# Chunk 0's denominators from one matmul, chunk 3's second score products halved on VectorE, a last column piece of 128, and a new order of the steps

## The chip, the cores and the metric

The kernel runs on one core of one Trainium2 chip. A core has five engines with queues of their own: TensorE (PE, matmuls, and PEld for its weight loads), VectorE (DVE), ScalarE (ACT), GpSimd (POOL) and SyncE (SP). The last two mainly issue transfers here; ACT issues one as well. The metric is device time in microseconds of one launch. Before the change it is 195.9 us, the median of three runs (195.79 to 197.63).

## The reference

One transformer layer over 2048 positions of width 512, all in bfloat16:

```
h  = x + Attn(layernorm(x))            # 32 heads of 16
h2 = h + MLP(layernorm(h))             # 512 -> 1376 -> 512
Attn: q,k,v = x @ wqkv;  each position sees 8 positions: itself and 2, 4, .. 14 back
      logits = q*k summed over a head's 16 numbers, times 1/4; softmax over the 8; sum of p*v; @ wo
MLP:  relu(x @ W_gate) * (x @ W_up) @ W_down
```

A position before the first one is masked out. The output is h2.

## The kernel before

The 2048 positions are cut into four chunks (0 to 3) of 512. Within a chunk a step has a name, which the plan's code gives it (the first argument of `add`); here it is written name/chunk, for instance pr1/3.

- **Norm and projections.** xst, xag, xxn and their like make the first layer norm, xtp transposes on PE (xtd by a transfer). qkv0 to qkv11 are the projections, four matmuls of 512 columns each (line 572), and qe0 to qe11 (line 580) copy the banks out on ACT. Chunk 0's first six are cut into qka, qkb, qkc.
- **Scores.** pr0 and pr1 (line 620; the digit is the half hf: the near four or the far four of the eight positions) multiply q by the shifted k on DVE, 128x4096 at a time: one such tile holds two of the four t (a head's 16 numbers lie as 4 partitions by 4 tiles t), four shifts each. There are two of them for each half. sc0 and sc1 (line 628) sum over a head's numbers with the 128x32 matrix `sel`, sixteen matmuls per half: four column groups of the array times four t. ex0 and ex1 (line 696) take exp on ACT, mk masks in chunk 0.
- **Denominators.** In chunks 1 to 3 (`DEN1`) es (line 728) adds the two halves' exponentials on DVE and den is one matmul with `same` (line 713); in chunk 0 den is two matmuls with `spread`, one for each half, that add up in the bank (line 716). dl and dr (lines 719, 722) are ln and exp(-x) on ACT, which make the reciprocal. In chunks 1 to 3 am0 and am1 (line 740) multiply the exponentials by it; in chunk 0 the division comes later (om, line 795).
- **Weighted sums.** bd0 and bd1 (line 756) spread the weights over the partitions, four transfers each, in SP's queue. mu0 to mu3 (line 788, in chunk 0 line 803) multiply by v on DVE, ta (line 831) adds the upper half to the lower by a transfer that POOL issues, in chunks 0 to 2; tree (lines 791, 825) adds the rest on DVE, in chunk 3 all of it.
- **Output projection and second norm.** wo0 to wo3 (line 867) are four matmuls for 128 positions each, rs (line 878; in chunk 0 line 876 on ACT) adds the residual, hsq, hrl, hre and hxn make the second layer norm, htp transposes on PE, htd by transfers in SP's queue.
- **MLP.** mm0 to mm4 (line 940) are the gate and up projections, four groups of four matmuls in each, mm5 (line 907) the last 96 columns. ue and ge (lines 944, 947) copy out on ACT, gu (line 968) multiplies on DVE, gtd transposes the last piece. dn0 to dn3 (line 990) are the down projections of 128 positions each, in two parts: hidden tiles 0 to 7, then 8 to 10. o (line 1003, on ACT for chunks 0 and 1: line 999) evicts them, os (lines 1009, 1027) stores them from SP's queue; in chunks 0 and 1 oa (line 1024) adds to the residual by a transfer of POOL's first.
- **The last block.** In chunk 3 the last 128 positions are computed in column pieces (`LASTC`, lines 975 to 978): columns 0 to 255 (dn3) and 256 to 511 (dn4). Only the very last piece is stored from ACT's queue (lines 1006 to 1009).

All banks of PSUM are one pool of eight (line 294), the 4096-wide tiles one of five, the `gr` and `up_sb` tiles two each.

**What sets the order.** Each call of `add` numbers a step in the order of creation, and `RANK[number]` (lines 18 to 57) is its rank: each engine does its steps in the order of rank (lines 119 to 123). The planner (`Plan.order`) walks these queues with a duration for each step and chooses which buffer a step takes; the program is then written out in that order. So every engine works strictly down its list, and a step that waits holds back all that stand behind it on its engine.

Of the kernel before, what the change touches and what calls it, by code (L numbers as in the profile page):

```python
# [17 lines left out]
RANK = [  # L18
# [38 lines left out]
]  # L57


# [33 lines left out]
class Plan:  # L93
# [9 lines left out]
    def add(self, key, *a, **k):  # L103
        op = Op(*a, **k)
        op.key = key
        op.seq = len(self.ops)
        if RANK:
            op.prio = RANK[op.seq]
        self.ops.append(op)
        for b in set(op.take) | set(op.use):  # L110
            b.left += 1
        return op
# [90 lines left out]
def kernel(  # L203
# [12 lines left out]
    Bsz, S, D = A_x.shape  # L216
# [5 lines left out]
    W = 8  # L222
    DIL = 2
    PADL = 16
    DEN1 = (1, 2, 3)
    BCD = {(0,0):"SSSS",(0,1):"SSSS",(1,0):"SSSS",(1,1):"SSSS",(2,0):"SSSS",(2,1):"SSSS",(3,0):"SSSS",(3,1):"SSSS"}
    PRE = ()
    PRD = ()
    PRH = {}
    ODA = (0, 1)  # L230
    LATE = "ud"
    NAB = 0
# [64 lines left out]
    V = nc.vector  # L297
# [94 lines left out]
    HSP = ()  # L392
    TMT = (0, 1, 2, 3)
    TTM, DTG, ATE = 0.0845, 0.35, 0.3
    LASTC = (D // 2,)

    LNA = ((0, 1, 0, 1), (0, 0, 0, 0))

# [156 lines left out]
    for tk in range(NCK):  # L555
# [50 lines left out]
        for hf in range(2):  # L606
            sc, ex = Buf(at_s), Buf(ex_s)
            scd, prd = [], []
            for t in range(0, NT, 2):
# [12 lines left out]

                hs = PRH.get((tk, hf, t))

# [62 lines left out]
            elif tk in MERGE:  # L687
                scd = [add(("sc%d" % hf, tk), "PE", (4 - sum((tk, hf, t) in PRH for t in (0, 2))) * MM + SW, lambda p=prd: [f() for _, _, f in p],
                           [a for a, _, _ in prd], apr, take=[sc], use=[b for _, b, _ in prd], lat=PEL)]
# [21 lines left out]
        def f_dn(exs=exs, dn=dn, tk=tk, es=None):  # L711
            if tk in DEN1:
                nc.tensor.matmul(dn.t[:], lhsT=(same if tk in EARLY else spread)[:], rhs=es.t[:], start=True, stop=True)  # L713
                return
            for hf in range(2):
                nc.tensor.matmul(dn.t[:], lhsT=(same if tk in EARLY else spread)[:], rhs=exs[hf].t[:], start=(hf == 0), stop=(hf == 1))  # L716
# [6 lines left out]

        if tk in DEN1:
            es = Buf(es_s)
# [250 lines left out]
        if tk == NCK - 1:  # L976
            cs = (0,) + LASTC + (D,)
            parts[-1:] = [(BPC - 1, a, b) for a, b in zip(cs, cs[1:])]
# [98 lines left out]
```

## Time and profile before

| what | value |
|---|---|
| median of three runs | 195.9 us |
| the profiled execution's own time | 196.0 us |
| its span | 193.7 us, at the full clock throughout |
| PE busy | 188.5 us (97%) |
| DVE busy | 147.2 us (76%) |
| ACT busy | 115.2 us (59%) |
| POOL busy | 17.4 us (9%) |

The span is what the profiler recorded; 2.3 us of the execution lie around it. The page cuts the span into 40 slices of 4.84 us. Busy shares are means over stages: the chain of waits says which engine's work ended last in each. A matmul's listed duration (379 ns for 512 columns) overlaps its neighbours'; what a matmul takes is read from a run of them in the chain. A vector instruction too is listed some 0.08 us longer than the distance to its successor.

### The profile page before, as it was taken

How to read it: one execution, taken by the hardware profiler on the slowest of the kernel's cores; microseconds unless marked ns; L12 is line 12 of the kernel's file. 1: busy time of each engine (PE TensorE's matmuls, PEld its weight loads, DVE VectorE, ACT ScalarE, POOL GpSimd, SP SyncE). 2: the span in 40 equal slices, each digit the busy share in tenths (PEclk: the TensorE clock that was granted, in tenths of full speed). 3: DMA queues.
4: the chain of work that ended last, by engine and by line, in shares of the span. 5: the costliest groups of instructions: out<-in, count | busy, mean ns of one | idle time of the engine just before them, and what ended most of it. 6: DMA issues, size and time to landing. Idle time of an engine off the chain costs nothing.

```text
span 193.7 us, 3083 instructions
## 1 busy us (share of the span) xinstructions
PE 188.5 (97%) x1120; PEld 99.0 (51%) x1139; DVE 147.2 (76%) x239; ACT 115.2 (59%) x241; POOL 17.4 (9%) x35
## 2 busy tenths in 40 slices
PE   7999999999999999999999999999999999999993
PEld 7986455555436435454444554444445444545452
DVE  6889999999999999999997679999564401134331
ACT  3489898965999673965156649623478712435500
POOL 3000002330000013100044001003000000000000
PEclk9999999999999999999999999999999999999999
DMA  6799564999902609917579974135101624001102
GB/s 205 242 296 376 138 155 93 192 196 260 353 5 49 171 14 199 191 33 170 122 143 194 180 192 90 29 80 94 18 0 27 162 58 135 0 27 54 30 23 86
DMA packets 25070, 24.61 MB, mean 127 GB/s; under 512 B 11136, under 2 KB 21344, under 8 KB 25056
## 3 DMA queue, kind: packets, MB, share of 16 engines
q1 hardware_dynamic: 22032, 16.23, 30.1%
q0 software_dynamic: 2304, 7.34, 20.8%
q10 hardware_dynamic: 720, 0.85, 1.2%
q8 instruction: 9, 0.15, 0.3%
q14 instruction: 5, 0.04, 0.1%
HBM read 8.42 MB, written 2.10 MB: 54 GB/s over the span
## 4 chain that ended last, share of the span: by engine, by line
PE 97%; ACT 1%; issue 1%; DVE 0%; ACTq 0%
PE bank L940 35%; PE bank L572 21%; PE bank L990 20%; PE bank L867 7%; PE bank L628 4%; PE bank L421 3%; PE bank L907 3%; PE bank L531 2%; PE bank L429 1%; ACT up_sb L944 1%; PE bank L870 0%; PE bank L713 0%; PE bank L716 0%; DVE row L1003 0%; ACT vT L580 0%
## 5 line engine op out<-in xcount | busy, mean ns | idle before, releaser
L940 PE MATMUL bank<-quad,wgu_sb 128*128 128x512 bf16 x312 | 72.4, 379 | 0.4
L940 PEld LDWEIGHTS <-wgu_sb 128*128 128x128 bf16 x320 | 31.0, 98 | 36.4 <-issue 1.0
L990 PE MATMUL bank<-wd_sb,gT 128*128 128x512 bf16 (+2 forms) x185 | 39.6, 366 | 0.1
L944 ACT CAST up_sb<-bank 128x512 bf16<-128x512 f32 x40 | 22.3, 590 | 22.2 <-PE bank L940 20.5
L572 PE MATMUL bank<-quad,wqk_sb 128*128 128x512 bf16 (+1 forms) x148 | 29.4, 344 | 0.3
L947 ACT ACTIVATE gr<-bank 128x512 bf16<-128x512 f32 x40 | 23.5, 606 | 9.5 <-PE bank L940 5.2
L968 DVE TENSOR_TENSOR gT<-gr,up_sb 128x1024 bf16<-128x1024 bf16 x20 | 13.8, 688 | 19.4 <-ACT up_sb L944 10.5
L990 PEld LDWEIGHTS <-gT 128*128 128x128 bf16 (+1 forms) x187 | 18.2, 98 | 19.8 <-DVE gT L968 0.2
L620 DVE TENSOR_TENSOR big<-quad,kT 128x4096 bf16<-128x4096 bf16 x12 | 27.2, 2284 | 0.2 <-ACT kT L580 0.2
L788 DVE TENSOR_TENSOR big<-big,vT 128x4096 bf16<-128x4096 bf16 x12 | 27.1, 2285 | 0.2 <-PE bank L940 0.2
L572 PEld LDWEIGHTS <-wqk_sb 128*128 128x128 bf16 x152 | 16.7, 113 | 10.3 <-issue 0.2
L831 POOL DMA_DIRECT2D big<-big x12 | 10.5, 904 | 81.7 <-DVE big L788 54.2
L791 DVE TENSOR_TENSOR big<-big 128x1024 bf16<-128x1024 bf16 (+2 forms) x24 | 16.9, 728 | 0.0
L572 PE MATMUL bank<-quad,wv_sb 128*128 128x512 bf16 x61 | 15.3, 380 | 0.2
L867 PE MATMUL bank<-wo_sb,quad 128*128 128x512 bf16 x62 | 15.0, 379 | 0.1
L1003 DVE TENSOR_TENSOR row<-x_sm,bank 128x512 bf16<-128x512 bf16 (+1 forms) x9 | 5.5, 627 | 12.2 <-PE bank L990 12.2
L456 ACT ACTIVATE row<-x_sm,mv 128x512 bf16<-128x512 bf16 x12 | 8.6, 718 | 7.2 <-DVE mv L448 7.1
L547 ACT COPY quad<-bank 128x1024 bf16<-128x1024 bf16 (+1 forms) x10 | 8.6, 898 | 7.2 <-PE bank L531 7.2
L878 DVE SCALAR_TENSOR_TENSOR x_sm<-x_sm,bank 128x512 bf16<-128x512 bf16 x12 | 8.2, 687 | 4.9 <-PE bank L867 4.7
L580 ACT CAST kT<-bank 128x512 bf16<-128x512 f32 x16 | 9.1, 597 | 3.3 <-PE bank L572 1.8
L467 DVE BATCH_NORM_STATS2 st<-x_sm 128x6 f32<-128x512 bf16 x16 | 10.2, 675 | 0.4 <-DMA x_sm<-in_A_x_dram 0.4
L580 ACT CAST quad<-bank 128x512 bf16<-128x512 f32 x16 | 9.5, 602 | 1.6 <-PE bank L572 1.5
(77 smaller groups left out, 169.5 us busy)
## 6 DMA issues: line engine op xcount, KB each, us to landing
big<-big POOLq DMA_DIRECT2D x12, 512.0 KB, 5.3
big<-ex SPq DMA_DIRECT2D x32, 128.0 KB, 2.8
wgu_sb<-in_B_W_gate_dram SPq DMA_DIRECT2D x2, 688.0 KB, 7.7
wgu_sb<-in_B_W_up_dram SPq DMA_DIRECT2D x2, 688.0 KB, 7.5
wd_sb<-in_B_W_down_dram SPq DMA_DIRECT2D x2, 640.0 KB, 7.9
x_sm<-in_A_x_dram SPq DMA_DIRECT2D x2, 512.0 KB, 5.1
x_sm<-up_sb POOLq DMA_DIRECT2D x4, 256.0 KB, 3.8
out_dram<-x_sm SPq DMA_DIRECT2D x4, 256.0 KB, 2.3
```

Of the source, the lines that this page charges most:

```text
L572: nc.tensor.matmul(mm.t[:, lo:hi], lhsT=wv_sb[:, dt, t:D:NT] if c == 2 else wqk_sb[:, dt, c * D + t:(c + 1) * D:NT], rhs=xnT.t[:, dt, lo:h ...
L580: nc.scalar.copy(out=o, in_=mm.t[:])
L620: V.tensor_tensor(out=pb.t[:].rearrange("p (t w) s -> p t w s", t=2), in0=q4, in1=k4, op=ALU.mult)
L788: V.tensor_tensor(out=mt.t[:], in0=ab.t[:], in1=v8, op=ALU.mult)
L791: V.tensor_tensor(out=mt.t[:, 0:n, :], in0=mt.t[:, 0:n, :], in1=mt.t[:, n:2 * n, :], op=ALU.add)
L831: nc.gpsimd.dma_start(mt.t[:, 0:4, :], mt.t[:, 4:8, :], accum_op=ALU.add)
L867: nc.tensor.matmul(od.t[:], lhsT=OT.t[:, t, j * P:(j + 1) * P], rhs=wo_sb[:, t, :], start=(t == 0), stop=(t == NT - 1 and tk not in RPE))
L940: nc.tensor.matmul(mm.t[:fs, lo:hi], lhsT=wgu_sb[:, dt, g, ft * P: ft * P + fs], rhs=hnT.t[:, dt, lo:hi], start=(dt == 0), stop=(dt == NT ...
L944: nc.scalar.copy(out=ub.t[:fs, i, :], in_=um.t[:fs, :])
L947: nc.scalar.activation(out=gr.t[:fs, i, :], in_=gm.t[:fs, :], func=ACT.Relu)
L968: V.tensor_tensor(out=gt.t[:fs, 0:n, :], in0=gr.t[:fs, 0:n, :], in1=ub.t[:fs, 0:n, :], op=ALU.mult)
L990: nc.tensor.matmul(od.t[:, c0:c1], lhsT=gts[ft].t[:fs, ft % 2, j * P:(j + 1) * P], rhs=wd_sb[:fs, ft, c0:c1], start=(ft == 0), stop=(ft == ...
```

## The change

Four things are set otherwise. `DEN1` now holds chunk 0: es/0 adds the two exponentials on DVE, and den/0 is one matmul. `PRH` marks both 4096-wide products of the far half in chunk 3: after each pr1/3 a new DVE step ph1/3 adds its upper 128x2048 half to its lower (lines 652 to 657), and sc1/3 then has eight matmuls in place of sixteen. `LASTC` gets a second cut: the last block's columns are made in pieces of 256, 128 and 128 (dn3, dn4, dn5); dn5's store goes out from ACT's queue, and dn4's, which did, now from SP's. There are 751 steps where there were 744, and `RANK` is a new list for them.

```
-    47, 51, 34, 38, 41, 43, 46, 50, 55, 44, 56, 69, 77, 64, 65, 76, 79, 48, 53, 60,
...
+    45, 49, 34, 38, 41, 43, 46, 50, 54, 72, 73, 75, 81, 47, 51, 63, 76, 53, 56, 58,
...
-    DEN1 = (1, 2, 3)
+    DEN1 = (0, 1, 2, 3)
...
-    PRH = {}
+    PRH = {(3, 1, 0): 'V', (3, 1, 2): 'V'}
...
-    LASTC = (D // 2,)
+    LASTC = (D // 2, 3 * D // 4)
```

The new ranks shuffle steps on all engines from the first projections on. Read out step by step, these are the places that matter below (the digit behind # tells the four groups of one mm, the two products of one half or the two parts of one dn apart):

| engine | before | after |
|---|---|---|
| PE | sc1/3 follows dn0/0 to dn3/0's first parts | sc1/3 follows all of dn/0, htp/1 and fourteen groups of mm/1; then mm5/1#2, mm1/1#3, mm5/1#1, den/3 |
| PE | nine groups of mm/2, then wo2/3, wo3/3, wo0/3, one mm, wo1/3 | fourteen groups of mm/2, mm5's two among them, then wo2/3, wo0/3, wo3/3, two mm, wo1/3 |
| PE | of chunk 3, ends dn0#1, dn1#1, dn2#1, dn0#2, dn1#2, dn2#2, dn4, dn3 | ends dn1#1, dn4#1, dn2#1, dn0#1, dn4#2, dn1#2, dn2#2, dn0#2, dn3, dn5 |
| DVE | pr1/3#2 amid chunk 1's trees, pr1/3#1 before hxn/1 | rs/1, mu0/2, hxn/1 (four), mu3, mu1, mu2 of chunk 2, pr1/3#2, tree3/2, ph1/3#2, tree3/2, gu2/1, pr1/3#1, ph1/3#1, tree0, tree2, gu3/1, es/3 |
| DVE | am0/3 and am1/3 almost together, then tree, gu, rs/2, mu2/3 | am0/3, rs2/2, rs0/2, gu1/1, am1/3, rs3/2, rs1/2, two gu5, hxn/2, mu0/3, gu4/1, mu2/3, mu3/3, mu1/3, then the trees with two gu5 |
| PE, ACT | qkv9/1 right behind den/0 and qe9/1 behind dl/0; qkv6/3 and qe6/3 both near the end of the projections; ex0/3 behind qe8/3, ge and ue of mm3/0 | qkv9/1 fourth of chunk 1 on PE, qe9/1 on ACT only behind qe0/2; qkv6/3 directly behind xtp/2, qe6/3 behind qe10/2; sc0/3 after seven groups of mm/0, ex0/3 behind ue4/0 |
| POOL | ta3/2 first, oa1/0 after the four ta/2 | oa1/0 first, then ta3/2, ta0/2, ta2/2, ta1/2 |
| SP | os0/2, os1/2 and os3/1 before gtd/3; at the end os0, os2, os1, os3 of chunk 3 | gtd/3, os3/2, os2/2, os4/3, os0/2, os1/2, os3/1, then os1, os2, os0, os3 of chunk 3 |

70 rows, old and new, of the table RANK are left out of this document.

## The prediction

> **What bounds the kernel now.** I read the head of the page first, then the chain of waits, then the windows, and only then single groups.
>
> ```profile
> span 193.7 us, 3083 instructions
> ...
> PE 188.5 (97%) x1120; PEld 99.0 (51%) x1139; DVE 147.2 (76%) x239; ACT 115.2 (59%) x241; POOL 17.4 (9%) x35
> ...
> DVE  6889999999999999999997679999564401134331
> ...
> PE 97%; ACT 1%; issue 1%; DVE 0%; ACTq 0%
> ```
>
> PE is 97% of the chain that ended last: nearly all of the span is matmuls end to end. VectorE is full for the first 27 slices (to about 131 us) and has room only behind them. So a change is worth what it takes from PE's list, plus the tail, minus what PE newly waits for. The chain in order of time gives the prices:
>
> ```profile
> 0.99 5.68 PE bank L421 x56
> ...
> 29.48 0.43 PE bank L716 x2
> ...
> 61.05 0.89 PE bank L531 x16
> ...
> 69.17 0.59 ACT up_sb L944
> ...
> 77.78 0.21 PE bank L713
> ...
> 95.06 0.98 PE bank L628 x16
> ...
> 138.74 2.59 PE bank L867 x12
> ...
> 149.76 0.66 PE bank L907 x8
> ...
> 181.11 9.56 PE bank L990 x55
> 190.66 0.02 issue
> 190.69 0.42 DVE row L1003
> ```
>
> A 512-column matmul takes 2.59 / 12 = 0.216 us, a 128-column one 0.89 / 16 = 0.056. PE works from 0.99 to 190.66, 189.7 us, and is busy for 188.5 of them: about 1.2 us of gaps in all, mostly pieces of 0.02 to 0.05 called issue. The worst stretch is here:
>
> ```profile
> 66.00:72.00 6.00, 5.85 (x51) 2.26 (x51) 5.78 (x3) 3.84 (x8) 0.86 (x1) 1.00 0.13 33
> ```
>
> PE (second number) is idle for 0.15 us of six, where the chain runs over ACT's copies. No reordering can bring more than these gaps; it can lose any amount.
>
> **The change part by part.** *Chunk 0's denominators:* two matmuls (0.43, line 716) become one (0.21, as line 713): −0.22 on PE. The new es/0 on VectorE costs what line 728 does:
>
> ```profile
> L728 DVE TENSOR_TENSOR row<-ex,ex 128x512 bf16<-128x512 bf16 x3 | 1.3, 419 | 0.0
> L722 ACT ACTIVATE rec<-lnd 128x512 bf16<-128x512 f32 x4 | 2.6, 650 | 0.1
> L719 ACT ACTIVATE lnd<-bank 128x512 f32<-128x512 f32 x4 | 2.5, 618 | 0.4 <-PE bank L713 0.4
> L990 PE MATMUL bank<-wd_sb,gT 128*128 128x256 bf16 x20 | 2.5, 272 | 0.0
> L1003 DVE TENSOR_TENSOR row<-x_sm,bank 128x512 bf16<-128x512 bf16 x7 | 4.6, 686 | 10.9 <-PE bank L990 10.9
> L1003 DVE TENSOR_TENSOR row<-x_sm,bank 128x256 bf16<-128x256 bf16 x2 | 0.8, 422 | 1.3 <-PE bank L990 1.3
> ```
>
> 0.42 us, 0.34 of it in distance to the next. PE's other projections cover it; were the cover gone, wo/0 would come 0.34 late.
>
> *sc1/3:* sixteen matmuls take 0.98. Four run side by side for 0.216, so four rounds are 0.86 and 0.12 is a lump. Halving saves 0.43 if the lump stays and 0.49 if it shrinks too; I take 0.43, as two rounds of the row. In the Trainium skill, TensorEngine Tiling (Array Packing), section Key Properties, says that changing the tiling mode drains TensorE. By that rule the lump is paid once per sc, so the saving would be 0.43; without it 0.49 and a sum 0.06 lower. Row and rule do not contradict, no run here separates them.
>
> *Two ph1/3:* 128x2048 adds on VectorE. Six products of that size are one row below, 6.89 us, so 1.15 each, 2.3 together. They lie beside PE's work if sc1/3 is asked for late enough; that is the main question:
>
> ```profile
> 13.39 6.89 DVE L637 TENSOR_TENSOR big<-quad,kT 128x2048 bf16<-128x2048 bf16 x6
> ...
> 90.53 0.08 DVE L878 DVE_READ_ACCUMULATOR x_sm<-x_sm,bank 128x1 f32 x1
> ...
> 90.92 2.28 DVE L620 TENSOR_TENSOR big<-quad,kT 128x4096 bf16<-128x4096 bf16 x1
> 93.12 1.38 DVE L502 TENSOR_SCALAR row<-x_sm,mv,rs 128x512 bf16<-128x512 bf16 x4
> 94.41 6.69 DVE L788 TENSOR_TENSOR big<-big,vT 128x4096 bf16<-128x4096 bf16 x3
> ...
> 117.85 2.28 DVE L788 TENSOR_TENSOR big<-big,vT 128x4096 bf16<-128x4096 bf16 x1
> ...
> 136.84 0.75 DVE L825 TENSOR_TENSOR quad<-big 128x512 bf16<-128x512 bf16 x2
> ```
>
> Chunk 1's last rs ends at 90.6, set by wo/1, whose place on PE hardly moves. From there the new VectorE list has, up to the end of the second ph1/3: four mu of 2.20 (8.8), four hxn (1.3), two pr1 of 2.20 (4.4), two ph1 (2.3), and two tree and one gu steps (about 1.8, from line 728's price and twice that): 18.6, so 109.2. PE asks for sc1/3 behind fourteen more mm groups (12.1), four second parts of dn/0 (2.6) and two htp (0.4), less 0.2 for den/0: 14.9 after 95.06, so 110.0. **Margin 0.8 us**: no wait.
>
> What follows sc1/3 is a chain: 110.6 its end; ex with its hop 111.4; es 111.8; PE reaches den/3 three groups (2.2 with two of 0.66 and one of 0.86) behind sc1/3, at 112.7; dl and dr, 1.27 by their rows, give 114.4. am0/3 goes at once, am1/3 behind rs2/2, rs0/2 and gu1/1 and ends near 117.5. bd1/3's four transfers stand in SP's queue behind it:
>
> ```profile
> 106.24 8.66 SPq L756 DMA_DIRECT2D big<-ex  x8
> ...
> L756 SPq DMA_DIRECT2D big<-ex x32: 543/566/2107, 20.4 to 114.3; - x32
> ...
> DMA to landing us min/median/max: 2.5/2.8/7.0
> ```
>
> Three issues of 0.57 and a landing of 2.8 behind the fourth's start: 122.0. The other steps ahead of mu0/3 on VectorE (rs, hnm, gu, hxn of chunk 2) end about then too. From 122.0 VectorE has four mu (8.8), four trees of about 2.1 (1.15, 0.6 and 0.34), gu4/1 and two gu5 (1.2): the last tree ends at 140.4. PE asks for wo2/3 behind three mm groups net (2.6) and mm5/2's two (1.3) more than before, less 0.65: 3.3 after 138.74, so 142.0. **Margin 1.6**; before, it was 138.74 − (136.84 + 0.75) = 1.1. Behind wo/3, mm/3 starts some 14 us after wo1/3 against 13.4 before, long enough for the four htd in SP's queue; chunk 3's gu and dn come in about the same distances. I find no new wait for data.
>
> *Last pieces:* dn4 and dn5 are 22 matmuls of 0.056, 1.23, for 11 of 0.108 (half of 0.216), 1.19: +0.04. The last add has 128 columns: 686 − 422 = 264 ns are 256 columns, so half as many save 0.13 of the 0.42 at the end. The last store has 32 KB:
>
> ```profile
> out_dram<-row SPq DMA_DIRECT2D x3, 128.0 KB, 1.7
> out_dram<-row ACTq DMA_DIRECT2D x1, 64.0 KB, 1.6
> out_dram<-row SPq DMA_DIRECT2D x1, 64.0 KB, 1.5
> ```
>
> 128 KB land in 1.7, 64 KB in 1.5 to 1.6: size hardly counts, so bounds of −0.1 and +0.2 (as slow as 128 KB), and I take 0, as the rows are nearest to it. The Trainium skill, DMA: Bandwidth & Descriptors, Specifications, puts full rate at 512 B or more and says that below this the engines read, modify and write. Rows of 256 B against 512 would fall under that; by it I should take the +0.2 end and 195.5 in all. No run of before has such a store.
>
> *The order:* the stretch at 66 to 72 loses its reason in part, since sc0/3's products are now done 1.8 us ahead, but ACT's copies are packed differently; I take ±0.
>
> Sum: −0.22 − 0.43 + 0.04 − 0.13 = −0.74 on the profiled execution's 196.0 (span 193.7 and 2.3 around it), so **195.3**. Its 196.0 lies 0.1 above the median of 195.9; I leave that in.
>
> **The rivals.**
>
> *Late weights for mu/3 (slower).* bd/3 sits on the chain above. If its landing took the 7.0 of the worst row in place of 2.8, mu0/3 would start 4.2 later, use up the 1.6 and hold wo2/3, and with it all of PE, for 2.6: 197.9, slower than before. It decides from a landing of 4.4 on. For it: the bd/3 of before were eight issues in 8.66 us, not 4.6. Against: then chunk 2's accumulating transfers were running (ta/2, last issued at 103.93 and landing in some 5.3, by the rows below); now they are issued some ten us ahead of bd/3.
>
> ```profile
> 103.93 0.86 POOL L831 DMA_DIRECT2D big<-big  x1 [1.68 <-DVE big L788]
> ...
> big<-big POOLq DMA_DIRECT2D x12, 512.0 KB, 5.3
> ...
> 80.64 1.56 ACT L944 CAST up_sb<-bank 128x512 bf16<-128x512 f32 x3
> ```
>
> *Banks held.* ACT works down its list, and the new one leaves three banks lying: qkv9/1's from about 25 to 51, qkv6/3's from 34 to 60, sc0/3's from 71 to 86. PE then lives on six or seven of eight banks, with a copy freed every 0.48 us ((1.56 − 0.59) / 2 in the last row, 0.59 being one). A matmul group lasts 0.86, so ACT is fast enough unless VectorE's gu holds it: `gr` and `up_sb` have two tiles each, and gu3/0 stands behind es/2. Two or three waits of 0.3 to 0.5 are +1.0: 196.3. Against it: the stretch of before that looked like this cost 0.15.
>
> *The stores at the end.* os4/3 waits for dn4/3, near 186.7, and os0/2, os1/2 and os3/1, 512 KB that left long before, now stand behind it on SP. From 186.8 on 1.05 MB leave (eight blocks of 128 KB in all) where 0.52 did. Between 186 and 194 the transfers of before reached this rate per slice of 0.2 us:
>
> ```profile
> GB/s 0 0 0 0 0 0 0 0 0 0 0 0 87 364 205 0 0 0 0 241 333 164 358 215 238 90 0 0 0 26 259 44 0 0 0 0 0 0 0 0
> ```
>
> At 364 GB/s 1.05 MB are 2.9 us, done before the last store is issued near 190.4. At 215 they are 4.9, to 191.7: the last store goes 1.3 later, 196.6.
>
> *Nothing is saved.* The matmuls taken out end up as gaps, because PE waits for the same thing after them: 195.9.
>
> **How the numbers follow.** Forecast 195.3 (194.8 to 195.6 by the bounds above): 0.50. Banks, 196.3 (195.6 to 197.2): 0.17. Stores, 196.6: 0.13. Nothing saved, 195.9: 0.08. Late weights, 197.9 (196 to 199): 0.10, most of it over the bound. Gain of more than 1.9: 0.02, since PE's list is only 0.6 shorter and the gaps 1.2. One per cent, 1.96 us, is what a measurement of this kernel can tell from no change, as the three runs before lie 1.8 apart. So faster 0.02, within 0.89, slower 0.09. The range goes from 194.7 to 197.1: it leaves out the upper half of the late weights, and a little at both ends.
>
> **What would show it.** Line 713 has four matmuls and line 716 none; line 628 has 120, and sc1/3 takes 0.55 at about 110 in the chain. The last 512-column matmuls end at about 189 and the last add starts near 190.1. VectorE's second ph1/3 ends before 110, its last tree of chunk 3 before 142. It is wrong if PE's windows show idle time of more than 0.3 us in any 6: near 77 it would be banks, near 110 the ph1, near 142 the weights; or if more than 3.0 us lie between the last matmul and the end, which would be the stores.

## The result, and the profile after

The changed kernel takes 198.53 us (median of 4 runs, 197.63 to 200.11) beside 195.84 for the kernel before: a ratio of 1.0115, 95% interval 1.0075 to 1.0154. In a second measurement, with 12 runs beside 23 (e9 below), the medians are 198.10 and 196.55, and the ratio is 1.0058 (1.0026 to 1.0090). Each ratio is taken from the fast runs alone and need not be the quotient of the medians beside it, which are of all runs. The change makes the kernel slower by 0.6 to 1.2%; the forecast of 195.3 and its range up to 197.1 were missed. The profiled execution took 197.63 us at full clock.

The page of the changed kernel, its head, PE's slices and the chain by engine:

```profile
span 195.6 us, 3078 instructions
...
PE 188.7 (96%) x1122; PEld 99.0 (51%) x1141; DVE 150.8 (77%) x243; ACT 115.0 (59%) x241; POOL 21.6 (11%) x35
...
PE   7999999999989999988999999999999999999994
...
PE 55%; DVE 16%; DMA 14%; issue 5%; ACT 3%; POOL 3%; SPq 1%; ACTq 0%; DVEq 0%; POOLq 0%
```

Before, 97% of the chain was PE; now it is 55%. The two dips in PE's row, at the twelfth slice and at the eighteenth and nineteenth, are the two waits that PE's timeline shows (start, duration, group, and in brackets the idle time ahead of it with what ended it):

```profile
58.42 0.38 PE L713 MATMUL bank<-row,same 128*128 128x512 bf16 x1 [0.54 <-DVE row L728]
...
87.14 0.38 PE L867 MATMUL bank<-wo_sb,quad 128*128 128x512 bf16 x1
89.00 3.41 PE L867 MATMUL bank<-wo_sb,quad 128*128 128x512 bf16 x15 [1.47 <-DVE quad L825]
```

The first is den/1, the second wo/1. A matmul that stands alone is listed with 0.38 where one in a run takes 0.216, so each wait costs 0.16 more than its idle time: 0.70 and 1.63. The chain says what lies behind the second, and where the changed steps ended up:

```profile
61.38 1.26 PE bank L531 x16
...
79.87 7.90 DMA big<-big
...
88.51 0.44 DVE quad L825
88.95 0.05 issue
89.00 3.41 PE bank L867 x15
...
112.73 0.54 PE bank L628 x8
...
192.79 0.02 issue
192.82 0.29 DVE row L1003
```

PE's last matmul ends at 192.79, before at 190.66: 2.13 later. PE's list is 0.62 shorter (0.22 and 0.44 saved, 0.04 added), so 2.75 of idle time is new: 0.70 at den/1, 1.63 at wo/1, 0.10 in the first 56 matmuls (5.78 us against 5.68), and 0.37 at chunk 0's sixteen transposes, htp/0 (1.26 us at 61.38, before 0.89 at 61.05). These make 2.80, 0.05 more than needed. Behind the last matmul 2.81 us are left in place of 3.04, and around the span 2.03 in place of 2.3. Together 2.13 − 0.23 − 0.27 = +1.63, which is 197.63 less 196.0.

**Why wo/1 waits.** The transfer in the chain is ta1/1, an accumulating one of 512 KB that POOL issues; tree1/1 waits for it, and wo/1 for tree1/1. In the kernel before, the rows of POOL's and SP's transfers by line, between 77.5 and 93 us, read (the three durations are shortest, median, longest):

```profile
L831 POOL DMA_DIRECT2D big<-big x1: 862/862/862, 78.5 to 78.5; - x1
...
DMA to landing us min/median/max: 5.5/5.5/5.5
...
L756 SPq DMA_DIRECT2D big<-ex x8: 543/556/566, 86.5 to 91.1; - x8
...
DMA to landing us min/median/max: 2.5/2.6/2.8
```

ta1/1 landed in 5.5 us, at 84.0, and the eight broadcasts bd/2 began at 86.5. The same rows for bd/2 in the changed kernel:

```profile
L756 SPq DMA_DIRECT2D big<-ex x8: 542/705/2107, 80.0 to 87.9; - x8
...
DMA to landing us min/median/max: 2.7/3.7/7.5
```

They begin 0.1 us behind ta1/1 and run beside it: ta1/1 takes 7.9 in place of 5.5, the worst of them 7.5 in place of 2.8. They begin there because am/2, which computes what they spread, has been moved up on VectorE. The row at 79.53 is am/2; the other rows of VectorE's timeline are used further on:

```profile
48.15 2.29 DVE L620 TENSOR_TENSOR big<-quad,kT 128x4096 bf16<-128x4096 bf16 x1 [0.24 <-POOL wd_sb L850]
51.09 2.29 DVE L620 TENSOR_TENSOR big<-quad,kT 128x4096 bf16<-128x4096 bf16 x1 [0.65 <-ACT kT L580]
...
79.53 0.76 DVE L740 TENSOR_TENSOR ex<-ex,rec 128x512 bf16<-128x512 bf16 x2
...
87.79 0.69 DVE L791 TENSOR_TENSOR big<-big 128x1024 bf16<-128x1024 bf16 x1 [1.91 <-DMA big<-big]
...
93.55 2.29 DVE L788 TENSOR_TENSOR big<-big,vT 128x4096 bf16<-128x4096 bf16 x1 [0.22 <-issue]
...
110.97 1.23 DVE L654 TENSOR_TENSOR big<-big 128x2048 bf16<-128x2048 bf16 x1
...
125.75 2.29 DVE L788 TENSOR_TENSOR big<-big,vT 128x4096 bf16<-128x4096 bf16 x1 [0.74 <-DMA big<-ex]
...
143.10 1.09 DVE L825 TENSOR_TENSOR quad<-big 128x512 bf16<-128x512 bf16 x3
```

The new list wants bd/2 early, because mu0/2, which needs it, now follows chunk 1's last rs at once; before, pr1/3#1 and hxn/1 stood between them (90.92 to 94.41). The last of VectorE's chunk 3 sums, the row at 143.10, ends at 144.2; the chain has wo/3 at 144.58.

**Why den/1 waits.** The waits of 0.24 and 0.65 in the two rows at 48 and 51 delay VectorE's list of products, at whose end es/1 stands: it starts at 57.95, before at 56.51. ScalarE's timeline shows what the second waits for:

```profile
50.47 1.07 ACT L580 CAST kT<-bank 128x512 bf16<-128x512 f32 x2 [1.97 <-DVE big L620]
```

The copy qe5/2 into kT has been put behind a product of chunk 1 that reads the same tile, and waits 1.97 us for it; VectorE's next product then waits 0.65 for qe5/2 in turn. The 0.37 at htp/0 lies behind es/1 on the same list: PE's weight loads for these transposes wait there for hxn/0 of VectorE.

```profile
61.60 0.87 PEld L531 LDWEIGHTS <-row 128*128 128x128 bf16 x12 [0.17 <-DVE row L502]
```

### The profile page after: what moved, and what is told of

It reads as the page before. It is cut to its first block, busy times and chain, and to the rows that moved or that the text cites. A ratio compares the mean times of both kernels' runs of the same rounds, so it can differ in the third digit from the quotient of the medians.

```text
span 195.6 us, 3078 instructions
## 1 busy us (share of the span) xinstructions
PE 188.7 (96%) x1122; PEld 99.0 (51%) x1141; DVE 150.8 (77%) x243; ACT 115.0 (59%) x241; POOL 21.6 (11%) x35
## 4 chain that ended last, share of the span: by engine, by line
PE 55%; DVE 16%; DMA 14%; issue 5%; ACT 3%; POOL 3%; SPq 1%; ACTq 0%; DVEq 0%; POOLq 0%
PE bank L940 26%; PE bank L990 18%; DMA big<-big 7%; PE bank L867 5%; DVE big L637 4%; DMA x_sm<-in_A_x_dram 4%; DVE big L788 4%; POOL wgu_sb L849 3%; DVE st L467 3%; DVE big L620 2%; PE bank L907 2%; DMA big<-ex 2%; DMA quad<-row 1%; PE bank L572 1%; ACT x_sm L876 1%
## 5 line engine op out<-in xcount | busy, mean ns | idle before, releaser
L940 PE MATMUL bank<-quad,wgu_sb 128*128 128x512 bf16 x312 | 71.6, 379 | 0.4
L990 PE MATMUL bank<-wd_sb,gT 128*128 128x512 bf16 (+3 forms) x194 | 39.0, 355 | 0.2
L572 PE MATMUL bank<-quad,wqk_sb 128*128 128x512 bf16 (+1 forms) x149 | 29.9, 345 | 0.2
L990 PEld LDWEIGHTS <-gT 128*128 128x128 bf16 (+1 forms) x198 | 18.4, 98 | 19.7
L1003 DVE TENSOR_TENSOR row<-x_sm,bank 128x512 bf16<-128x512 bf16 (+2 forms) x10 | 5.6, 580 | 10.4 <-PE bank L990 10.4
L867 PEld LDWEIGHTS <-quad 128*128 128x128 bf16 x64 | 6.2, 98 | 9.3 <-DVE quad L825 2.0
L502 DVE TENSOR_SCALAR row<-x_sm,mv,rs 128x512 bf16<-128x512 bf16 x24 | 8.7, 405 | 2.4 <-ACT rs L484 1.8
```

The lines of the kernel that those rows point to most:

```text
L572: nc.tensor.matmul(mm.t[:, lo:hi], lhsT=wv_sb[:, dt, t:D:NT] if c == 2 else wqk_sb[:, dt, c * D + t:(c + 1) * D:NT], rhs=xnT.t[:, dt, lo:h ...
L867: nc.tensor.matmul(od.t[:], lhsT=OT.t[:, t, j * P:(j + 1) * P], rhs=wo_sb[:, t, :], start=(t == 0), stop=(t == NT - 1 and tk not in RPE))
L940: nc.tensor.matmul(mm.t[:fs, lo:hi], lhsT=wgu_sb[:, dt, g, ft * P: ft * P + fs], rhs=hnT.t[:, dt, lo:hi], start=(dt == 0), stop=(dt == NT ...
L990: nc.tensor.matmul(od.t[:, c0:c1], lhsT=gts[ft].t[:fs, ft % 2, j * P:(j + 1) * P], rhs=wd_sb[:fs, ft, c0:c1], start=(ft == 0), stop=(ft == ...
```

## The experiments

In all diffs `behind(ref, *steps)` gives the steps the ranks right behind ref's on their engine's list; the planner then chooses the buffers anew. A comment behind # names the runs that have the line. Where a run adds steps or takes some out (e4, e6, e7, e8, e11, e15), further lines, not shown, give new steps their place and let all others keep their ranks.

**The late spots put back.** am/2 behind tree1/1, where the kernel before has it, then qe5/2 ahead of the wait, then both:

```diff
+    behind(('tree1', 1), ('am1', 2), ('am0', 2))     # e1_am_back, e3_both
+    behind(('qe4', 2), ('qe5', 2))                   # e2_qe_back, e3_both
```

> The changed kernel, but am1/2 and am0/2 stand on VectorE behind chunk 1's last tree step again, as in the kernel before, so that bd1/2 and bd0/2 (eight transfers) start when ta1/1's transfer has landed. Theory A, the eight broadcasts and ta1/1's accumulating transfer share the DMA engines and ta1/1 lands in 7.9 us in place of 5.3: it lands in 5.8 or less, VectorE's wait of 1.9 on it is gone, wo/1 starts near 87, the run takes 195.6 to 196.2. Rival B, VectorE's list itself is late (gu0/0 and gu2/0 wait for ACT ahead of the trees): only the 0.7 of the two am steps are won, 197.0. Rival C, POOL's descriptors are written late because VectorE holds the memory port: the landing stays at 7.9 and the time at 197.6.

> The changed kernel, but qe5/2 stands on ACT directly behind qe4/2, ahead of pr0/1#2. Theory: the wait of ACT for pr0/1#2 (2.0 us) and of pr1/1#2 for qe5/2 (0.65) go, es/1 ends 0.7 earlier, PE's wait of 0.5 at den/1 goes, and PE's lag there falls from 1.2 to 0.5 or 0.6; the collision further on stays: 196.9 to 197.2. Rival, VectorE's lateness comes from POOL's copies behind ta2/0 and from bd/0 (0.24 and 0.63 us): den/1 waits as before, 197.6.

> Both moves, am/2 back on VectorE and qe5/2 up on ACT. If the two causes add up: 195.0 to 195.4, that is 2.3 to 2.7 less than the changed kernel and 0.5 to 0.9 less than the kernel before, as forecast blind for a change without new waits. If something else is left, 195.9 or more.

Beside 196.74 for the kernel before: e1_am_back 199.6, ratio 1.0120 (1.0066 to 1.0174); e2_qe_back 197.39, 1.0040 (1.0018 to 1.0061); e3_both 198.72, 1.0098 (1.0082 to 1.0115). In PE's timeline of e2_qe_back the wait at den/1 is gone and the one at wo/1 stays:

```profile
88.19 3.41 PE L867 MATMUL bank<-wo_sb,quad 128*128 128x512 bf16 x15 [1.34 <-DVE quad L825]
```

In that of e3_both both are gone, and another is there (e1_am_back has it too, with 2.12 us, beside den/1's 0.54):

```profile
87.58 3.62 PE L867 MATMUL bank<-wo_sb,quad 128*128 128x512 bf16 x16
...
95.73 3.42 PE L990 MATMUL bank<-wd_sb,gT 96*128 96x512 bf16 x15 [2.38 <-DMA gT<-row]
```

ta1/1 landed in 7.8 us in e2_qe_back and in 5.5 in e3_both, so am/2's place sets the landing, as theory A has it; by rival C it would have stayed at 7.9. Both causes of the waits are shown, but not the gain that was expected from their removal: with am/2 back gtd/0 comes late, as it stands behind bd/2's eight issues in SP's queue (87.74 to 92.83), and dn/0's second parts want gT. The changed order asks for it 1.7 us behind wo/1, with eight matmuls between; the kernel before asked 6.8 us behind (89.88 to 96.64), with 24 matmuls, sc1/3 and htp/1 between.

**The collision, alone.** The kernel before with eight more 128 KB broadcasts on SP, issued behind bd1/1 from `rec` of chunk 2 into `wqk_sb`, whose weights are no longer needed:

```diff
+        if tk == 2:
+            def f_xt(rc=rc):
+                for i in range(8):
+                    nc.sync.dma_start(wqk_sb[:, i // 2, i % 2 * CS:(i % 2 + 1) * CS], rc.t[0:HB, :].unsqueeze(1).to_broadcast([HB, 4, CS]))
...
+            add(("xt", tk), "SP", 4.6, f_xt, [rcd], 0, use=[rc], lat=1.0)
...
+    behind(('bd1S', 1), ('xt', 2))
```

> The kernel before, with eight more broadcasts of 128 KB from the reciprocal of chunk 2 (known at 79.8) into the unused projection weights, in SP's queue ahead of bd0/2: nothing waits for them, the output is the same. Theory A: they run beside ta1/1's transfer (issued at 78.5), its landing grows from 5.2 to 7 or more, tree1/1 and wo/1 come 1.5 to 2.5 late, 197.0 to 198.0. Rivals B and C: the transfers cost nothing, 195.9.

197.67 against 196.74, ratio 1.0044 (1.0020 to 1.0069). ta1/1, issued 1.33 us ahead of the first of them, landed in 6.2 us where it took 5.5, less than the 7 or more expected, and wo/1 did not wait. The eight held SP's queue to 88.67, so bd/2 and all behind it came later, and ta1/2 met bd/3, which began 1.13 us behind it (2.31 in the kernel before, where ta1/2 landed in 6.1). The chain of that run:

```profile
106.27 7.87 DMA big<-big
114.13 0.02 issue
114.16 0.69 DVE big L803
114.85 0.68 DVE quad L837 x2
115.53 0.05 issue
115.57 2.33 PE bank L879 x10
```

The same 7.9 us a chunk later, with the same followers up to wo/2. Taken together, such a transfer, the last of its chunk's four, landed in 5.5 us with no broadcasts inside, in 6.1 when they began 2.31 us behind its start, in 6.2 at 1.33, and in 7.9 at 1.13 and at 0.1. The distance alone doesn't set it: in the 6.1 and in the 7.9 of this run oa1/0's 256 KB were under way as well.

**am/2 between the two.** Behind gu1/0, at 85.24 where the changed kernel has 79.53 and e3_both 87.30, with qe5/2 as in e2_qe_back:

```diff
+    behind(('gu1', 0), ('am1', 2), ('am0', 2))
+    behind(('qe4', 2), ('qe5', 2))
```

> The changed kernel with qe5/2 up on ACT and with am1/2 and am0/2 on VectorE behind gu1/0, some 4 us later than in the changed kernel and 3 earlier than in the run with both moves. Theory, the place of am/2 is squeezed from both sides: early, bd/2 runs beside ta1/1 and wo/1 waits; late, gtd/0 stands behind bd/2 in SP's queue and dn/0's second parts wait for it. In the middle ta1/1 lands in 6.5 or less, wo/1 starts without a wait, gtd/0 lands before 92, and the run takes 0.3 to 0.9 less than the kernel before. Rival, the new list has no place for it, since mu0/2 needs bd/2 by 93 and gtd/0 is needed by 91.5: one of the waits stays with 1 us or more, the run takes as long as the kernel before or longer.

197.27 against 196.55, ratio 1.0051 (1.0028 to 1.0074), as the rival had it. ta1/1 lands in 5.5 us again, PE's wait at wo/1 is 0.15, but mu0/2 waits for bd/2 on VectorE, and PE waits for gT:

```profile
93.89 2.29 DVE L788 TENSOR_TENSOR big<-big,vT 128x4096 bf16<-128x4096 bf16 x1 [1.78 <-DMA big<-ex]
...
94.32 3.42 PE L990 MATMUL bank<-wd_sb,gT 96*128 96x512 bf16 x15 [0.97 <-DMA gT<-row]
```

**The parts alone, in the kernel before's order.** The second cut (e6), chunk 0's single matmul (e7), and the two additions right behind their products (e8):

```diff
+    LASTC = (D // 2, 3 * D // 4)                      # e6_last_pieces
+    DEN1 = (0, 1, 2, 3)                               # e7_one_den
+    PRH = {(3, 1, 0): 'V', (3, 1, 2): 'V'}            # e8_halved_early
```

> The kernel before with the last block in pieces of 256, 128 and 128 columns alone; dn5 behind dn3 on PE, o5 behind o3, os4 in SP's queue behind os1/3, os5 last on ACT. By the terms of the prediction: +0.04 on PE, 0.13 less for the last add, 0 for the store: 0.1 less than the kernel before. Rival, a store with rows of 256 B is slow: 0.1 to 0.3 more.

> The kernel before with chunk 0's denominators from one matmul alone; es/0 on VectorE ahead of mu1c/0, behind chunk 2's statistics. By the term of the prediction 0.22 less, since PE's list is shorter by one matmul and no wait is new. Rival, the 0.34 on VectorE shifts mu/0 and with it wo/0, whose first matmul started 0.2 behind its last om: 0 to 0.2 more.

> The kernel before with the two halving adds alone, each right behind its pr1/3 in the old order, so that sc1/3 is asked for at 95 and VectorE is full ahead of it. Term of the prediction: 0.43 less on PE. But 2.3 us more of VectorE before hxn/1 and mu/2 shift the trees of chunk 2: wo/2 had a margin of some 1.5, and sc1/3 had waited for the second pr1: I expect PE to wait 1 to 2 us at sc1/3, htp/1 or wo/2, so 0.5 to 1.5 more than the kernel before. Rival, VectorE's own idle time behind es/3 (2.6 us up to 110) takes it up: 0.4 less.

Beside 196.55: e6 196.32, ratio 1.0013 (0.9988 to 1.0039); e7 196.62, 1.0014 (0.9992 to 1.0035); e8 198.34, 1.0097 (1.0069 to 1.0124). The first two can't be told from no change, as their intervals hold 1. e6's span ends 2.74 us behind the start of the last add, as the changed kernel's does (2.78), against 3.01 before: that part of the gain is real, though too small for the medians. The halving costs 1.8 us where it has no room; PE's timeline of e8 shows one of its waits, for a gu step that stands behind the additions:

```profile
85.63 1.90 PE L995 MATMUL bank<-wd_sb,gT 128*128 128x512 bf16 x8 [0.98 <-DVE gT L973]
```

**The changed kernel again, with three moves, and without the halving.**

```diff
+    behind(('gu1', 0), ('am1', 2), ('am0', 2)); behind(('qe4', 2), ('qe5', 2))   # e10_three_moves
+    behind(('ta1', 2), ('oa1', 0))
+    r = [o.prio for o in plan.ops if o.key == ("dn3", 0)][0]
+    for i in range(3):
+        [o for o in plan.ops if o.key == ("dn%d" % i, 0)][1].prio = r + 0.1 + 0.1 * i
...
-    PRH = {(3, 1, 0): 'V', (3, 1, 2): 'V'}                                     # e11_no_halving
+    PRH = {}
```

> The changed kernel unaltered, beside the two kernels below on the same chip. Theory (two late spots, TensorE idle for some 0.75 us around den/1 and htp/0 and for some 2.0 us at wo/1, against 0.60 us of list saved): 2.0 to 2.3 us above the kernel before on the same chip, a ratio of 1.010 to 1.012, with the wait of 1.3 to 1.5 us ahead of wo/1's second matmul and of about 0.5 ahead of den/1's in the waits of TensorE. Rival (the start of the program, which differs by up to a microsecond between executions, makes the difference): a ratio within 1.005.

> The changed kernel with its late spots taken out: am/2 on VectorE behind gu1/0, as in e5_am_middle, qe5/2 on ScalarE ahead of pr0/1's wait, as in e2_qe_back, and the gates' transfer gtd/0 given some 3.5 us more, since three of TensorE's second parts of dn/0 go behind dn3/0's first part. Theory: no wait over 0.2 us at den/1, at wo/1 and at dn/0, so the 0.97 us that e5_am_middle still waited for gT are gone too: 0.7 to 1.2 us below e5_am_middle's distance to the kernel before, that is a ratio of 0.997 to 1.002, and 2 us below e9_after_again. Rival (the order is late everywhere, and a wait that is removed comes back behind the next step): again 1.003 to 1.008, with a wait at wo/2 or sc1/3 in place of the one at dn/0.

> The changed kernel in its own order, without the two ph1/3: VectorE does 2.3 us less, TensorE's sc1/3 is sixteen matmuls again (0.98 us in place of 0.54). Theory (the two additions lie in VectorE's room and cost nothing, the loss is in the order): 0.4 to 0.5 us above e9_after_again, a ratio to the kernel before of 1.012 to 1.015, with the same waits at den/1 and wo/1. Rival (the additions on VectorE are what made it late): below e9_after_again by 0.5 to 2 us, a ratio of 1.000 to 1.008.

Beside 196.55: e9 198.10, ratio 1.0058 (1.0026 to 1.0090), lower than expected, with the same two waits (0.55 and 1.08). e10 202.30, 1.0243 (1.0199 to 1.0287): both theories missed. The dn parts that I moved away had covered hxn/1, and their place shows it in PE's timeline:

```profile
96.54 0.93 PE L531 MATMUL bank<-identity,row 128*128 128x128 bf16 x8 [2.81 <-DVE row L502]
```

e11 198.94, 1.0100 (1.0064 to 1.0136), with the waits at den/1 (0.38) and wo/1 (1.24) still there: 0.84 above e9 in the medians, where 0.4 to 0.5 was expected if the additions cost nothing; the intervals overlap. Without the additions the loss is no smaller, so they don't make it.

**hxn/1 ahead of mu0/2**, with e10's moves (e12) and with e5's alone (e13):

```diff
+    behind(('hnm', 1), ('hxn', 1))
```

> e10_three_moves with one more step moved: VectorE's four hxn/1, 1.3 us, go ahead of mu0/2, into the 2.0 us in which VectorE waits for bd/2. Theory (in e10_three_moves the 2.81 us ahead of htp/1 are only hxn/1 standing behind mu0/2 in VectorE's list): that wait goes, hxn/1 ends at about 92.5 where TensorE asks at 93.7, and the 0.77 us behind it go too; 3.0 to 4.0 us below e10_three_moves, a ratio of 1.003 to 1.009 to the kernel before, or below. Rival (bd/2 landing late moves all of VectorE's list, whoever goes first): the wait moves to sc1/3 or wo/2 and the ratio stays above 1.012.

> e5_am_middle with hxn/1 ahead of mu0/2, the second parts of dn/0 left where the changed kernel has them. Theory (TensorE's 0.97 us for gT in e5_am_middle hang on SyncE's queue, not on VectorE): the wait for gT stays at 0.8 to 1.1 us, and the ratio stays at 1.003 to 1.007. Rival (VectorE's 1.78 us of waiting for bd/2 are what is left of the loss): the ratio falls to 1.000 or below.

Beside 196.48: e12 202.35, 1.0319 (1.0275 to 1.0362), a miss again, though the ratio is above 1.012 as the rival had it; one of its six executions took 403.80 us, which stays unexplained. hxn/1 started at 94.06 where 91.2 was expected: VectorE's timeline puts 1.88 us of waiting ahead of it down to ScalarE's rs, the statistics of the second norm, and e13 shows the same with 1.87. And oa1/0, moved behind ta1/2, landed in 8.53 us beside the ta/2 and kept `up_sb` from ScalarE, 2.95 us of waiting for PE at 114.81. e13 197.77, 1.0048 (1.0016 to 1.0080), the ratio as expected, with a longer wait for gT (1.55).

**gtd/0 between bd1/2 and bd0/2** on SP's queue, on e13, with the halving (e14) and without it (e15):

```diff
+    behind(('bd1S', 2), ('gtd', 0))                   # e14_gates_ahead, e15_gates_no_halving
-    PRH = {(3, 1, 0): 'V', (3, 1, 2): 'V'}            # e15_gates_no_halving
+    PRH = {}
```

> e13_hxn_and_gates with gtd/0 put on SyncE's queue between bd1/2 and bd0/2, four transfers earlier, so that gT lands at about 92 in place of 94.3 to 94.6, ahead of the 93.3 at which TensorE asks for it; bd0/2 ends some 1.2 us later. Theory (VectorE's list from the landing of bd/2 on is what bounds the changed kernel): mu0/2 starts at about 95.0 and the second ph1/3 ends some 17.4 us later, at 112.4, as in e5_am_middle (93.89 to 112.54 with 1.3 us of hxn in it); TensorE now asks for sc1/3 at about 111.7 and waits 0.5 to 0.9 us there: the wait moves and the ratio stays at 1.003 to 1.007. Rival (separate late spots): the wait for gT goes and none comes in its place, ratio 0.997 to 1.001.

> e14_gates_ahead without the two ph1/3, so that sc1/3 is sixteen matmuls again. Theory (VectorE bounds from bd/2 on): its list is 2.3 us shorter ahead of sc1/3, the second pr1/3 ends at about 110.2, TensorE doesn't wait at sc1/3 and spends 0.43 us more in it; 0.1 to 0.5 us below e14_gates_ahead in spite of the longer list of TensorE. Rival (TensorE's list bounds, and the additions lie in room): 0.4 us above e14_gates_ahead.

Beside 196.57: e14 197.57, ratio 1.0060 (1.0022 to 1.0098); e15 197.00, 1.0028 (1.0004 to 1.0051). In PE's timeline of e14 the wait for gT is gone, and sc1/3 waits:

```profile
112.70 0.62 PE L628 MATMUL bank<-big,sel 128*32 128x512 bf16 x8 [0.96 <-DVE big L654]
```

VectorE's timeline of e14 has no gap from hxn/1, which waited for ScalarE, to there:

```profile
94.00 1.38 DVE L502 TENSOR_SCALAR row<-x_sm,mv,rs 128x512 bf16<-128x512 bf16 x4 [1.88 <-ACT rs L484]
95.30 8.89 DVE L788 TENSOR_TENSOR big<-big,vT 128x4096 bf16<-128x4096 bf16 x4
104.22 2.29 DVE L620 TENSOR_TENSOR big<-quad,kT 128x4096 bf16<-128x4096 bf16 x1
...
111.42 1.23 DVE L654 TENSOR_TENSOR big<-big 128x2048 bf16<-128x2048 bf16 x1
```

In e15, 2.3 us less on VectorE, PE asks for sc1/3 and gets it:

```profile
110.66 1.05 PE L628 MATMUL bank<-big,sel 128*32 128x512 bf16 x16
```

This is the pair that says most. Removing PE's wait for gT gained nothing (e5, e13 and e14 lie at 1.0051, 1.0048 and 1.0060), for VectorE's list then sets sc1/3. What starts that list is not bd/2's landing alone. In e5 mu0/2 waits for bd/2 until 93.89; in e14 bd/2's last transfer, issued at 91.7, had landed by 94.5, and mu0/2 started at 95.30 because hxn/1, put ahead of it, waited for ScalarE until 94.00. Where VectorE's list is shortened at the price of a longer one on PE, the kernel is 0.57 us faster in the medians; the two intervals overlap, and the reading rests on the waits in the profiles.

No version came out ahead of the kernel before. What keeps e15 0.3% above it stays open in part. Its profile has no wait of PE's over 0.2 us, but htp/0 takes 1.23 us there against 0.89, and the chains of the other runs in the changed order that list these sixteen transposes whole have 1.22 to 1.26; in every run in the order of the kernel before it is 0.89. No run here moves hxn/0 ahead. The profiled execution of e15, 196.07, is also the shortest of its twelve, 0.07 above the profiled one of the kernel before, so the waits of its longer ones are not seen.

## Why the prediction was wrong, step by step

- **The step that failed** is the start of VectorE's list at sc1/3: "Chunk 1's last rs ends at 90.6, set by wo/1, whose place on PE hardly moves. From there the new VectorE list has, up to the end of the second ph1/3 … 18.6, so 109.2." The list was right: from 93.55 it took 18.6, to 112.2. Its start was wrong: the last rs ended at 93.1, as wo/1 had waited 1.63 for ta1/1 and PE was 0.9 late ahead of that already. PE, held by the same waits, came to sc1/3 at 112.73 where 110.0 was forecast, and did not wait. So the margin there, 0.5 for 0.8, held because both sides were late, which was luck; the loss lay ahead of it.

  What the step left out is when the data of its first reader land. mu0/2 stands first in the list and needs bd/2, and by the rows of before bd/2's last transfer was issued at 91.1 and landed 2.6 to 2.8 later, near 93.8. The kernel before did pr1/3#1 and hxn/1 in that time, as the rows at 90.92, 93.12 and 94.41 in the prediction's own fence show; the change takes that cover away. Either mu0/2 starts at 94, and sc1/3 is late by 2.6 (112.6 where PE asks at 110.0), or bd/2 goes earlier and runs beside ta1/1. The order given does the second; e3 and e5 do the first, where mu0/2 waits 3.15 and 1.78 us for bd/2. I counted each instruction between the two ends and asked of none when its data land.
- **"I find no new wait for data"** fell with it, at wo/1 (1.63), den/1 (0.70) and htp/0 (0.37). The second came from the copies' order on ScalarE, which "±0" had passed over; what is late at htp/0, hxn/0, stands behind es/1 on the same list. None of the three lies near 77, 110 or 142, where the prediction looked for idle time.
- **The rival of late weights** had the mechanism, SP's broadcasts meeting POOL's accumulating transfers, but put it at bd/3's landing and 2.6 us; here bd/2 met ta1/1, and PE waited for ta1/1, 1.63. That the rival's 197.9 lies near the measured time is chance. bd/3 landed in 2.5 to 3.0 (2.8 assumed), for ta/2 was far ahead, as the prediction said. Its sum for VectorE's chunk 3 was right too: from mu0/3 to the last tree 18.4 forecast (122.0 to 140.4) and 18.4 measured (125.75 to 144.2). The margin at wo/3, 1.6 forecast, was 0.4. The 194.8 to 195.6 around the forecast is wider than the bounds given for it (0.1 and 0.06 down, 0.2 up).
- **Right:** den/0 is one matmul (−0.22); sc1/3 takes 0.54 in place of 0.98 (−0.44, forecast −0.43); the last add 0.29 in place of 0.42 (−0.13). sc1/3's lump over two rounds of 0.216 is 0.11, before 0.12 over four: the lump does not shrink with the rounds and is paid once per sc, as the drain at a change of mode in the Trainium skill, TensorEngine Tiling (Array Packing), Key Properties, would have it.
- **The last stores:** the tail shrank by 0.23, of which the add is 0.13, so the store gave 0.10, the lower of its bounds. The Trainium skill's 512 B rule (DMA: Bandwidth & Descriptors, Specifications) would have cost 0.2 by the prediction's estimate; neither this run nor e6 shows any of it. The rival of the stores at the end didn't come.
- **Banks held** and **nothing saved** were not it: the matmuls taken out are gone from PE's list, and no bank is named in a wait of PE's over 0.2 us.
- The 0.27 us less around the span I had not counted. It is 2.3 us in e6 and e7, 1.8 in e8, which has the halving in the old order, and 2.0 in e11, which has the new order without the halving. So the halving and the order each go with less; why stays open.

## What to carry to other kernels

When a step is taken out from between a transfer and its reader, ask of the reader first when its data land: the instructions that stood there were the transfer's cover. On an engine that is full, a list's length is not its end; write the landing time of each operand beside the step that reads it, and keep broadcasts from starting beside an accumulating transfer on which the path waits. A wait removed ahead of the engine that bounds comes back at that engine: try which list bounds by shortening it at the other's cost, as e15 does.

## What the hardware showed that I had not expected

- **Two queues share the engines.** Of the four 512 KB accumulating transfers of POOL's in chunk 1 of the kernel before, the first, alone, landed in 4.5 us, the others, each begun while the one ahead was still under way, in 5.2 to 5.5. The last one took 6.2 with eight 128 KB broadcasts on SP from 1.33 us behind it (e4), and 7.9 with eight from 0.1 us behind it (7.87 in e4 a chunk later, with oa1/0 under way too). The Trainium skill, DMA: Bandwidth & Descriptors, Queues, rings and completion order, says that each DMA engine goes round the queues that have work; these landings agree, though they show only that transfers of two queues slow each other.
- **A copy of four numbers took 5 us.** POOL's timeline, before:

```profile
41.08 0.60 POOL L849 COPY wgu_sb<-big 1x4 bf16<-1x4 bf16 x1 [1.60 <-DVE big L791]
```

and after:

```profile
42.89 5.08 POOL L849 COPY wgu_sb<-big 1x4 bf16<-1x4 bf16 x1 [3.08 <-DVE big L791]
```

It ended at 47.97, where VectorE's row of two-input operations from 42.74 on paused, and VectorE's next product waited 0.24 for POOL. The Trainium skill, SBUF — State Buffer, Who interferes with whom, says that a VectorE instruction with two inputs in SBUF contends with a GpSimd instruction that reads SBUF. That agrees with the place. The copy took 5.08 us in eleven of the twelve profiles of the changed order, 0.60 in all five of the order before, and 2.20 in e11 (43.09 to 45.29), the length of the one product beside it. Why it is mostly held through several instructions and not just one, no run here explains, and the profile's spans on POOL are rough.
- **The start moves.** PE's first transposes began between 5.6 and 6.9 us in the profiled executions, by when the input landed; the twelve that began by 6.4 have waits of 0.15 to 0.7 on PE between 7 and 36 us (1.13 and 1.65 in two), the five that began from 6.5 on have none over 0.2. The runs of one kernel spread by 1 to 3 us; how much of that is the start was not tried.
